# A fused attention and two-MLP kernel: the MLP part in a written order, one stream of weight steps, and shifted tile addresses

## The chip, the cores and the metric

One core of a Trainium2 chip runs the whole kernel in one launch. The metric is the device time of an execution in microseconds; the median of several executions is what counts. The profile shows one execution.

## The reference

```python
# attention: q, k, v are (2, 8, 768, 64); 4 sink columns, window 128
scores = q @ k^T / 8, kept where the column is a sink or 0 <= row - column < 128
a = softmax(scores);  x = a @ v, laid out as (1536, 512)
# first MLP: w_in (512, 2048), w_out (2048, 512)
h = x @ w_in;  g = h * sigmoid(1.702 * h);  x = g @ w_out
# second MLP: w_gate, w_val (512, 1536), w_out (1536, 512)
out = (sigmoid(x @ w_gate) * (x @ w_val)) @ w_out
```

The weights come as 64-bit floats in DRAM. The kernel reads them as pairs of 32-bit words.

## The kernel before, in words

**Three products for one.** Every MLP product is made in fp32r (a 32-bit type that TensorE takes in one pass) from a high and a low part: `mm3` (lines 147 to 151) issues hi by hi, hi by lo and lo by hi into one PSUM bank. A sum over the 512 contracted elements is 4 calls of `mm3`, 12 matmuls of 128 x 128 by 512 columns. This text calls such 12 matmuls a sum, and 4 sums (48 matmuls, one block by 512 tokens) a stage.

**Blocks.** The hidden width is walked in blocks of 512, the 1536 tokens in three blocks `tb` of 512. The first MLP has blocks i0, o0 to i3, o3 (`w_in`, `w_out`), the second g0, v0, p0 to g2, v2, p2 (`w_gate`, `w_val`, `w_out`): 17 blocks of four rows, 68 rows. A stage of an i-block is called h, of an o-block y, of a p-block o. In h, y, g and v stages the weights are the stationary operand; in o stages they are the moving one and the activations are stationary.

**A row of weights** (`weight_steps`, lines 104 to 131): a DMA of 512 KB into `raw` (two buffers); ACT takes the absolute value with a scale and an accumulator (line 118); DVE shifts (121), merges the sign (123) and the low bits (125); ACT casts to the high part `wh` (128); POOL subtracts to get the low part `wl` (130). The load of row i+2 is issued behind line 125 of row i, which frees its buffer.

**Where the blocks lie.** `load_w` gives block number k (in the order i0, o0, i1, o1, ..., p2) a buffer of `wpool` on the left side of SBUF where k mod 5 is 0 or 1, of `wpool2` on the right side otherwise. In the program as built, `wpool` begins at a multiple of 128 bytes of a partition. The right side is filled downwards: pool `acc` (29,344 bytes) begins at byte 200,000, which is 64 past a multiple of 128, and so do `tmp` below it and all tiles of `wpool2`. The blocks that lie in `wpool2` are i1, o1, i2, o3, g0, v0, v1, p1 and g2.

**Activations.** Behind an h sum ACT takes the sigmoid, DVE multiplies (line 461), ACT casts to `gh` (451), DVE subtracts to `gl` (453). A y stage uses them as the moving operand; DVE adds the sum into `yacc` (487). Behind a g and a v sum come a sigmoid (662), a multiplication (663) and the same split.

**The order.** The attention part runs under a manual schedule: strings `ORDER0` (units 0 to 9) and `ORDER` (from unit 10) say in which order the parts of a unit are issued, with a lag in units behind each letter. T transposes q and k, t copies the result to `kq`, S are scores, m the masked maximum, x the exponential, n the normalisation, P transposes probabilities and p copies them, K, k do so for the sinks, V multiplies with v, h and l split the result into `xh`, `xl`, H is a piece of the first h product, G a step of its activation, Y a sum of y, W a part of the weight steps, D a few dummy matmuls. T, P and K share a PSUM pool of two buffers (`ps_t`). A string `TAIL` orders the transition. From there the MLP part is left to the framework's scheduler, which orders the instructions of each engine by its own estimate.

**Stages.** `h_stage` makes its first sum, then calls `after`, which runs the y stage of the token block before, and goes on with its other three sums. `gv_stage` does the same with the o stage behind its first g and v sums.

Of the kernel before, what the change touches and what calls it, by code (L numbers as in the profile page):

```python
# [27 lines left out]
TAIL = "G4 H4 Y1 H4 G4 Y1 H4 G4 Y1 H4 G4 Y1 W3 G3 W3 Y1 G3 W3 Y1 G4 W4 Y1 G4 W4 G4 W4 G4"  # L28
I_FULL = 10
LOADS = (2, 3)  # L30
W_SEQ = [0, 0, 1, 3, 3, 3, 3, 3, 3, 3, 1]
# [22 lines left out]
def fast_path(ctx, tc, ident, nwv, any_, q, k, v, n_sink, window, w_in, w_out, w_gate, w_val, w_out2, out):  # L54
# [39 lines left out]
    def weight_block(src, nm, pool):  # L94

        wh = pool.tile([P, 4, 512], F32R, tag="wh", name=f"wh_{nm}")
        wl = pool.tile([P, 4, 512], F32R, tag="wl", name=f"wl_{nm}")

        def load(i):
            raw = stg.tile([P, 512, 2], I32, tag="raw", bufs=2, name=f"raw_{nm}_{i}")  # L100
            nc.sync.dma_start(raw, src[:, i, :].bitcast(I32).rearrange("p (f t) -> p f t", t=2))
            return raw, wh[:, i, :], wl[:, i, :], f"{nm}_{i}"

        return (wh, wl), [lambda i=i: load(i) for i in range(4)]

    def weight_steps(loads):


        raws = [load() for load in loads[:2]]
        yield  # L110
        for i in range(len(loads)):
            raw, h, l, nm = raws[i]
            lo, hi = raw[:, :, 0], raw[:, :, 1]
            w = stg.tile([P, 512], I32, tag="w", bufs=2, name=f"w_{nm}")
            wf = w.bitcast(F32)
            n = len(nbig)
            nbig.append(nm)
            nc.scalar.activation(wf, hi.bitcast(F32), AF.Abs, scale=2.0 ** -112,
                                 accum_out=big[:, n : n + 1])
            yield  # L120
            nc.vector.tensor_scalar(w, w, 3, None, ALU.logical_shift_left)
            yield
            nc.vector.scalar_tensor_tensor(w, hi, -0x80000000, w, ALU.bitwise_and, ALU.bitwise_or)
            yield
            nc.vector.scalar_tensor_tensor(w, lo, 29, w, ALU.logical_shift_right, ALU.bitwise_or)
            raws += [load() for load in loads[i + 2 : i + 3]]
            yield
            nc.scalar.copy(h, wf)  # L128
            yield
            nc.gpsimd.tensor_tensor(l, wf, f32(h), ALU.subtract)  # L130
            yield

    slots = [0]

    def load_w(src, nm):

        w = weight_block(src, nm, wpool if slots[0] % 5 < 2 else wpool2)
        slots[0] += 1
        return w
# [63 lines left out]
    wz = acc.tile([P, 512 + 16], mybir.dt.bfloat16, name="wz")  # L203
# [220 lines left out]
    def mlp_h():  # L424


        for g in range(len(blocks)):
            tb, off = divmod(g * QB, TB)
            ts_ = slice(off, off + QB)
            for f2 in range(GF // 2):  # L430
                pool, tag = h_banks[(g * GF // 2 + f2) % len(h_banks)]
                ps = pool.tile([P, 2, QB], F32, tag=tag, name=f"ha_{g}_{f2}")
                for i in range(2):
                    f = 2 * f2 + i
                    fs = slice(f * P, (f + 1) * P)
                    for kk in range(KD):
                        mm3(ps[:, i, :], wi[0][:, kk, fs], wi[1][:, kk, fs],
                            xh[tb][:, kk, ts_], xl[tb][:, kk, ts_], kk == 0, kk == KD - 1)
# [7 lines left out]
    def split(nm, src):  # L446
# [5 lines left out]
        yield  # L452
# [12 lines left out]
    def at_once(steps):  # L465
        while True:
            try:
                next(steps)
# [8 lines left out]
    def y_part(g, tb, wo, gs, d):  # L477
# [5 lines left out]
        ya = yacc[:, d, tb * TB : (tb + 1) * TB]  # L483
        if g == 0:
# [3 lines left out]


    first = [load_w(src, nm) for src, nm in ((in_block(w_in, 0), "i0"), (out_block(w_out, 0), "o0"))]  # L490
    wi = first[0][0]
    w_steps = weight_steps([load for _, loads in first for load in loads])
# [5 lines left out]
    W_ALL = 1 + 4 * 6  # L498
    w_done = [1]

    def w_some(n):
        piece(w_steps, n)
        w_done[0] += n
# [11 lines left out]

    parts = {"c": t_prev, "T": t_mm, "t": t_out, "S": s_mm, "m": s_max, "x": s_exp, "i": s_inv, "n": s_norm,
# [6 lines left out]
    piece(w_steps, 1)  # L523
# [3 lines left out]
    wo = first[1][0]  # L527

    def y0_steps():
        for tb in range(NTB):  # L530
            for d in range(KD):
                y_part(0, tb, wo, gs0[tb], d)
# [18 lines left out]
    with tc.manual_schedule(engines=engines):  # L551
        i = 0
        while nxt["l"] < len(units):
# [13 lines left out]
            for o in orders[which]:  # L567
                if o[0] == "H":

                    h_some(int(o[1:]), l_done // NPAIR if w_done[0] >= W_ALL else 0)  # L570
# [8 lines left out]
                elif o[0] == "W":  # L579
                    steps = W_SEQ[i] if i < len(W_SEQ) else 3  # L580
# [8 lines left out]
            if i == len(units):  # L589
                esq.close()  # L590
                g_pools.append(ctx.enter_context(tc.tile_pool(name="gpb", bufs=4)))
# [5 lines left out]
        piece(w_steps, 99)  # L597
# [5 lines left out]
        wpool2 = ctx.enter_context(tc.tile_pool(name="wpool2", bufs=3, side="right"))  # L603
        second = load_w(in_block(w_in, 1), "i1")
        w_steps = weight_steps(second[1])
        for o in TAIL.split():
            if o[0] == "H":
                h_some(int(o[1:]), len(blocks))
            elif o[0] == "W":
                piece(w_steps, int(o[1:]))  # L610
# [4 lines left out]
        for _ in h_steps:  # L615
            pass
        esg.close()
        for steps in (w_steps, silu0, y0):
            for _ in steps:
                pass  # L620
    ps_h = ctx.enter_context(tc.tile_pool(name="ps_h", bufs=4, space=PSUM))

    def load_w2(src, nm):
        w, loads = load_w(src, nm)
        for _ in weight_steps(loads):
            pass
        return w

    def h_stage(g, tb, wi, after):
        res = []  # L630
        for f in range(GF):
            ps = ps_h.tile([P, TB], F32, tag="h", name=f"h_{g}_{tb}_{f}")
            fs = slice(f * P, (f + 1) * P)
            for kk in range(KD):
                mm3(ps, wi[0][:, kk, fs], wi[1][:, kk, fs], xh[tb][:, kk, :], xl[tb][:, kk, :],
                    kk == 0, kk == KD - 1)
            res.append(at_once(silu_steps(g, tb, f, ps)))
            if f == 0:
                after()
        return res  # L640

    def y_stage(g, tb, wo, gs):
        for d in range(KD):
            y_part(g, tb, wo, gs, d)
            ya = yacc[:, d, tb * TB : (tb + 1) * TB]
            if g == NG1 - 1:
                nc.scalar.copy(xh[tb][:, d, :], ya)
                nc.vector.tensor_tensor(xl[tb][:, d, :], ya, f32(xh[tb][:, d, :]), ALU.subtract)

    def gv_stage(g, tb, wg, wv, after):  # L650
        res = []
        for f in range(GF):
            fs = slice(f * P, (f + 1) * P)
            pss = []
            for w, nm in ((wg, "g"), (wv, "v")):
                ps = ps_h.tile([P, TB], F32, tag="h", name=f"{nm}_{g}_{tb}_{f}")
                for kk in range(KD):
                    mm3(ps, w[0][:, kk, fs], w[1][:, kk, fs], xh[tb][:, kk, :], xl[tb][:, kk, :],
                        kk == 0, kk == KD - 1)
                pss.append(ps)  # L660
            sg = tmp.tile([P, TB], F32, tag="sg", name=f"sv_{g}_{tb}_{f}")
            nc.scalar.activation(sg, pss[0], AF.Sigmoid)  # L662
            nc.vector.tensor_tensor(sg, pss[1], sg, ALU.mult)  # L663
            res.append(at_once(split(f"v{g}_{tb}_{f}", sg)))
            if f == 0:
                after()
        return res

    oacc = acc.tile([P, NT // P, DM], F32, tag="yacc", name="oacc")

    def o_stage(g, tb, wo, gs):
        for j in range(TB // P):
            n = tb * (TB // P) + j
            ts_ = slice(j * P, (j + 1) * P)

            nd = 2 if g == NG2 - 1 and n == NT // P - 1 else 1
            for ds in (slice(i * DM // nd, (i + 1) * DM // nd) for i in range(nd)):
                ps = ps_y.tile([P, DM // nd], F32, tag="y", name=f"o2_{g}_{tb}_{j}_{ds.start}")
                for f in range(GF):
                    mm3(ps, gs[f][0][:, ts_], gs[f][1][:, ts_], wo[0][:, f, ds], wo[1][:, f, ds],  # L680
                        f == 0, f == GF - 1)
                oa = oacc[:, n, ds]
                if g == 0:
                    nc.scalar.copy(oa, ps)
                else:
                    nc.vector.tensor_tensor(oa, ps, oa, ALU.add)
                if g == NG2 - 1:
                    nc.sync.dma_start(out[n * P : (n + 1) * P, ds], oa)

    def check_inputs():  # L690

        fl = const.tile([P, 5], F32, name="fl")
        flag = const.tile([P, 1], F32, name="flag")
# [214 lines left out]
```

## Time and profile before

| what | value |
|---|---|
| median of 3 executions | 694.38 us (692.54 to 694.4) |
| profiled execution | 692.46 us |
| its span, first to last instruction | 690.7 us |
| PE busy in the span | 671.1 us (97%) |
| DVE, ACT, POOL busy | 395.3, 280.1, 154.1 us |
| DMA, mean rate | 71 GB/s |

PE is TensorE's matmul row. Matmuls are pipelined: one is shown as busy for about 0.39 us while the next starts 0.23 us behind it, so a busy PE says only that no gap opened. How fast it went is read from how many matmuls start in a stretch.

### The profile page before, as it was taken

The page shows a single profiled execution, that of the slowest core. Times are in us where ns is not written, and L with a number is a line of the kernel's source. Part 1 is how long each engine was busy: PE and PEld are TensorE (multiplying, and loading weights), DVE is VectorE, ACT ScalarE, POOL GpSimd, SP SyncE. Part 2 cuts the span into 40 slices and gives each one's busy share as a digit, 9 for nine tenths or more (in the row PEclk, how much of TensorE's full clock was granted, in tenths as well). Part 3 has the DMA queues.
Part 4 walks back from the last instruction along what each step waited for, and adds up shares of the span by engine and source line. Part 5 has one row for each costly group of instructions (what it writes and reads, how often), then busy time and mean ns, then how long its engine had stood idle before and what let it go on. Part 6 is the DMA issues. An engine that isn't in the chain of part 4 may idle for free.

```text
span 690.7 us, 9435 instructions
## 1 busy us (share of the span) xinstructions
PE 671.1 (97%) x3518; PEld 542.6 (79%) x3518; DVE 395.3 (57%) x792; ACT 280.1 (41%) x667; POOL 154.1 (22%) x235
## 2 busy tenths in 40 slices
PE   7899999999998999999999999999989999999996
PEld 3568888988886887888888888888868888888885
DVE  6987876567988889348856940206672325222222
ACT  4777766735535444234434532225441113111110
POOL 4656564103333331013102300003420002000000
PEclk9999999999999999999999999999999999999999
DMA  9855610013334434003300320002440000000101
GB/s 198 203 122 124 171 49 3 1 31 121 123 122 131 144 95 149 0 1 123 121 1 29 124 91 1 1 0 66 150 150 0 1 1 0 1 31 31 46 16 65
DMA packets 50150, 49.06 MB, mean 71 GB/s; under 512 B 39728, under 2 KB 39984, under 8 KB 50096
## 3 DMA queue, kind: packets, MB, share of 16 engines
q1 hardware_dynamic: 49264, 48.24, 24.3%
q8 instruction: 29, 0.48, 0.3%
q10 hardware_dynamic: 832, 0.13, 0.1%
q14 instruction: 25, 0.20, 0.1%
HBM read 45.22 MB, written 3.15 MB: 70 GB/s over the span
## 4 chain that ended last, share of the span: by engine, by line
PE 70%; DVE 15%; DMA 8%; ACT 4%; issue 2%; POOL 1%; SPq 0%; ACTq 0%; POOLq 0%; DVEq 0%
PE g L149 4%; PE o L149 4%; PE g L150 4%; PE o L151 4%; PE g L151 4%; PE o L150 4%; PE v L151 4%; PE v L150 4%; PE v L149 4%; PE o L408 4%; PE y L150 3%; PE y L151 3%; PE y L149 3%; PE s L314 3%; PE h L150 3%; PE h L151 3%
## 5 line engine op out<-in xcount | busy, mean ns | idle before, releaser
L663 DVE TENSOR_TENSOR sv<-v,sv 128x512 f32<-128x512 f32 x36 | 24.8, 689 | 114.4 <-PE v L151 114.3
L150 PE MATMUL y<-gl,wh_o 128*128 128x512 f32 x192 | 76.1, 397 | 1.3 <-DVE gl L453 1.3
L151 PE MATMUL y<-gh,wl_o 128*128 128x512 f32 x192 | 75.6, 395 | 0.0
L149 PE MATMUL y<-gh,wh_o 128*128 128x512 f32 x192 | 73.6, 398 | 1.7 <-ACT gh L451 1.7
L149 PE MATMUL o<-wh_p,gh_v 128*128 128x512 f32 (+1 forms) x148 | 57.0, 385 | 1.7 <-ACT gh_v L451 1.7
L662 ACT ACTIVATE sv<-g 128x512 f32<-128x512 f32 x36 | 21.5, 596 | 90.1 <-PE g L151 90.1
L150 PE MATMUL o<-wl_p,gh_v 128*128 128x512 f32 (+1 forms) x148 | 56.9, 384 | 0.0
L149 PE MATMUL g<-xh,wh_g 128*128 128x512 f32 x144 | 56.8, 394 | 0.0
L151 PE MATMUL v<-xh,wl_v 128*128 128x512 f32 x144 | 56.8, 394 | 0.0
L151 PE MATMUL o<-wh_p,gl_v 128*128 128x512 f32 (+1 forms) x148 | 56.7, 385 | 0.0
L150 PE MATMUL v<-xl,wh_v 128*128 128x512 f32 x144 | 56.7, 394 | 0.0
L151 PE MATMUL g<-xh,wl_g 128*128 128x512 f32 x144 | 56.7, 394 | 0.0
L150 PE MATMUL g<-xl,wh_g 128*128 128x512 f32 x144 | 56.7, 394 | 0.0
L149 PE MATMUL v<-xh,wh_v 128*128 128x512 f32 x144 | 56.7, 394 | 0.0
L151 PE MATMUL h<-xh,wl_i 128*128 128x512 f32 x144 | 56.7, 394 | 0.0
L150 PE MATMUL h<-xl,wh_i 128*128 128x512 f32 x144 | 56.7, 394 | 0.0
L149 PE MATMUL h<-xh,wh_i 128*128 128x512 f32 x144 | 56.7, 393 | 0.0
L451 ACT CAST gh_v<-sv 128x512 fp32r<-128x512 f32 x36 | 22.3, 620 | 79.0 <-DVE sv L663 78.8
L340 ACT ACTIVATE pr<-pr,nmax 128x272 f32<-128x272 f32 (+2 forms) x96 | 47.1, 494 | 15.1 <-DVE nmax L328 10.4
L355 POOL TENSOR_SCALAR pr<-pr,st 128x272 f32<-128x272 f32 (+2 forms) x96 | 44.5, 479 | 35.9 <-DVE st L346 19.8
L130 POOL TENSOR_TENSOR wl_p<-w_p,wh_p 128x512 fp32r<-128x512 f32 x12 | 16.4, 1372 | 153.9 <-ACT wh_p L128 153.9
L149 PEld LDWEIGHTS y<-gh,wh_o 128*128 128x128 f32 x192 | 36.5, 190 | 10.7 <-ACT gh L451 2.7
(138 smaller groups left out, 1465.8 us busy)
## 6 DMA issues: line engine op xcount, KB each, us to landing
raw_i<-in_moe_w_in_dram SPq DMA_DIRECT2D x16, 512.0 KB, 3.8
raw_o<-in_moe_w_out_dram SPq DMA_DIRECT2D x16, 512.0 KB, 3.3
raw_g<-in_moe_w_gate_dram SPq DMA_DIRECT2D x12, 512.0 KB, 3.4
raw_v<-in_moe_w_val_dram SPq DMA_DIRECT2D x12, 512.0 KB, 3.5
raw_p<-in_moe_w_out_dram SPq DMA_DIRECT2D x12, 512.0 KB, 3.2
v<-in_v_dram SPq DMA_DIRECT2D x12, 256.0 KB, 4.2
out_dram<-oacc SPq DMA_DIRECT2D x11, 256.0 KB, 2.0
k<-in_k_dram SPq DMA_DIRECT2D x10, 256.0 KB, 4.8
```

Of the source, the lines that this page charges most:

```text
L130: nc.gpsimd.tensor_tensor(l, wf, f32(h), ALU.subtract)
L149: nc.tensor.matmul(ps, ah, bh, start=first, stop=False)
L150: nc.tensor.matmul(ps, ah, bl, start=False, stop=False)
L151: nc.tensor.matmul(ps, al, bh, start=False, stop=last)
L314: nc.tensor.matmul(ss[j][:, :n], kq[p][hd, qsl], kq[p][hd, c0 : c0 + n], start=True, stop=True)
L340: nc.scalar.activation(pt, pt, AF.Exp, bias=nm[:, it : it + 1], scale=-1.0, accum_out=sts[u][:, 0, e, j : j + 1])
L355: nc.gpsimd.tensor_scalar(pt, pt, st[:, 1, e, j : j + 1], 1.0, ALU.mult, ALU.mult)
L408: nc.tensor.matmul(o[64 * j : 64 * j + 64, cs], vf(j), pf(j), start=i == 0, stop=i == len(steps) - 1)
L451: nc.scalar.copy(h, src)
L662: nc.scalar.activation(sg, pss[0], AF.Sigmoid)
L663: nc.vector.tensor_tensor(sg, pss[1], sg, ALU.mult)
```

## The change

- The MLP part is issued under the manual schedule too: `products_b` with `h_stage`, `y_stage`, `gv_stage`, `o_stage` is written out in the order in which the four engines get it.
- One generator, `weight_stream`, holds the steps of all 68 rows in order. `behind()` is called behind every sum (one call a sum) and advances it by 1, 1, 1, 2 groups in turn; a row has three groups. A block gets its buffer when block k-5 has been read, and the stream waits for that by yielding.
- From the tail on, the low part is subtracted on DVE (`SUB_B`), one row late.
- Behind an h sum the weight group stands between the cast to `gh` and the subtraction to `gl`. `h_stage` calls `after` behind its second sum.
- Blocks lie in five slots: two in `wpool`, one in the new `wpool3` (left side, opened when q and k are done), two in `wpool2`. i1 starts within the attention part.
- `wz` grows by 64 bytes, the tiles `st` from 64 to 128 bytes.
- `ORDER`, `ORDER0`, `TAIL`, `I_FULL` and `W_SEQ` change.

```diff
-ORDER = "W0 i-2 c-0 n-2 S0-1 S1-1 m0-1 m1-1 G2 x0-1 V-4 h-4 T-0 Y1 t-0 H1 l-4 P0-3 H1 W1 p0-3 P1-3 p1-3 H1 x1-1 K-3 k-3 W2 G2 H1"
-ORDER0 = "c-0 i-2 n-2 S0-1 S1-1 m0-1 m1-1 W0 x0-1 V-4 h-4 T-0 t-0 l-4 H1 P0-3 p0-3 W1 P1-3 p1-3 K-3 H1 H1 H1 x1-1 D4 k-3 W2"
-I_FULL = 10
+ORDER = "W0 S0-1 i-2 c-0 n-2 S1-1 m0-1 m1-1 G2 x0-1 V-4 h-4 T-0 Y1 t-0 P0-3 H1 H1 W1 p0-3 P1-3 l-4 p1-3 H1 x1-1 K-3 W2 k-3 G2 H1"
+ORDER0 = "c-0 i-2 n-2 D4 S0-1 S1-1 m0-1 m1-1 W0 x0-1 V-4 h-4 P0-3 T-0 t-0 l-4 H1 p0-3 W1 P1-3 p1-3 K-3 H1 H1 H1 x1-1 W2 k-3"
+TAIL = "G2 W1 G2 H8 G2 W1 G2 H4 W1 Y1 G2 W1 G2 H4 W1 Y1 G2 W1 G2 H4 W1 Y1 G2 W1 G2 H4 W1 Y1 G2 W1 G2 H4 W1 Y1 G3 W1 G1 Y1 G3 W1 G1 Y1 G3 W1 G1 Y1 G3 W1 G1"
+W_DRAIN = 4
+W_B = (1, 1, 1, 2)
+SUB_B = lambda nc: nc.vector
+I_FULL = 9
...
+    def weight_stream(blocks):
...
+        for n, (k, i) in enumerate(rows):
+            nm = blocks[k][0]
+            raw, w = raws.pop(n), ws[n]
+            lo, hi = raw[:, :, 0], raw[:, :, 1]
+            if n and late:
+                sub(n - 1)
+                yield n, False
             nc.vector.tensor_scalar(w, w, 3, None, ALU.logical_shift_left)
+            yield n, False
             nc.vector.scalar_tensor_tensor(w, hi, -0x80000000, w, ALU.bitwise_and, ALU.bitwise_or)
+            yield n, True
             nc.vector.scalar_tensor_tensor(w, lo, 29, w, ALU.logical_shift_right, ALU.bitwise_or)
+            load(n + 2)
+            yield n, True
+            if i == 0:
+                while k % 5 not in dict(w_pools) or (k >= 5 and blocks[k - 5][0] not in w_read):
+                    yield None
+                pool = dict(w_pools)[k % 5]
+                weights[nm] = [pool.tile([P, 4, 512], F32R, tag=t, name=f"{t}_{nm}") for t in ("wh", "wl")]
+            nc.scalar.copy(weights[nm][0][:, i, :], w.bitcast(F32))
+            late = sub_engine[0] is nc.vector
+            if not late:
+                yield n, False
+                sub(n)
+                yield n + 1, False
+            size(n + 1)
+            yield n + (not late), True
...
-    wz = acc.tile([P, 512 + 16], mybir.dt.bfloat16, name="wz")
+    wz = acc.tile([P, 512 + 48], mybir.dt.bfloat16, name="wz")
...
-            sts[u] = ap_.tile([P, 2, 2, 4], F32, tag="st", bufs=3, name=f"st_{nid(u)}")[:, :, :, :2]
+            sts[u] = ap_.tile([P, 2, 2, 8], F32, tag="st", bufs=3, name=f"st_{nid(u)}")[:, :, :, :2]
...
         nc.scalar.copy(h, src)
-        yield
+        yield "hi"
         nc.vector.tensor_tensor(l, src, f32(h), ALU.subtract)
...
+                if next(steps) == "hi":
+                    behind()
...
+        if 0 < g < NG1 - 1:
+            behind()
...
+    def behind():
+        w_group(W_B[sums[0] % len(W_B)])
+        sums[0] += 1
...
+            res.append(at_once(silu_steps(g, tb, f, ps)))
+            if f == (GF - 1 if (g, tb) == (1, 0) else 1):
+                after()
...
+                if nm == "g":
+                    nc.scalar.activation(sg, ps, AF.Sigmoid)
+                    behind()
+            nc.vector.tensor_tensor(sg, ps, sg, ALU.mult)
+            res.append(at_once(split(f"v{g}_{tb}_{f}", sg)))
+            if f == 0:
+                after()
...
-        wpool2 = ctx.enter_context(tc.tile_pool(name="wpool2", bufs=3, side="right"))
+        g_pools.append(ctx.enter_context(tc.tile_pool(name="gpb", bufs=4)))
+        wpool2 = ctx.enter_context(tc.tile_pool(name="wpool2", bufs=2, side="right"))
+        w_pools += [(3, wpool2), (4, wpool2)]
+        sub_engine[0] = SUB_B(nc)
...
+        products_b()
```

## Rows read from the trace of the kernel before

**Rows 1.** Page, part 1: busy time and instructions of each engine.

```profile
PE 671.1 (97%) x3518; PEld 542.6 (79%) x3518; DVE 395.3 (57%) x792; ACT 280.1 (41%) x667; POOL 154.1 (22%) x235
```

**Rows 2.** Windows, three stretches: busy (instructions) of PE, PEld, DVE, ACT, POOL; clock; DMA.

```profile
0.00:53.00 53.00, 44.56 (x353) 29.40 (x354) 41.37 (x163) 34.79 (x117) 30.26 (x77) 1.00 0.76 171
...
137.40:371.50 234.10, 231.12 (x1022) 188.29 (x1021) 172.34 (x252) 103.14 (x210) 50.95 (x36) 0.99 0.27 86
371.50:690.70 319.20, 311.00 (x1359) 252.93 (x1357) 121.63 (x178) 82.77 (x158) 32.27 (x24) 1.00 0.13 44
```

**Rows 3.** Windows of PE, undisturbed stages: y(o2), h(i3), h(i2), o(p0), o(p1).

```profile
286.25:297.15 10.90, 10.90 (x50) 1.00 0.00 0
319.10:329.98 10.88, 10.88 (x49) 1.00 0.43 143
252.08:263.28 11.20, 11.20 (x50) 1.00 0.44 115
410.70:421.60 10.90, 10.90 (x49) 1.00 0.01 2
545.80:556.80 11.00, 11.00 (x50) 1.00 0.00 0
```

**Rows 4.** The same view, stages with a wait: y(o1), y(o2), o(p1).

```profile
213.80:229.66 15.86, 13.39 (x50) 0.89 0.43 137
263.30:275.05 11.75, 11.24 (x50) 1.00 0.51 147
510.30:523.57 13.27, 11.54 (x49) 1.00 0.23 80
```

**Rows 5.** The same view, one sum of g1 between sums of v1.

```profile
493.70:496.45 2.75, 2.75 (x13) 1.00 0.42 167
```

**Rows 6.** Waits of PE: waiter, releaser, us in total, times, longest.

```profile
PE tp L370 <- DVE kq L301: 4.5, 8, 1.2
PE o L149 <- ACT gh_v L451: 1.7, 1, 1.7
```

**Rows 7.** Windows of PE: the stretch behind the wait at 214 us.

```profile
217.66:221.08 3.42, 3.42 (x8) 0.50 0.35 109
```

**Rows 8.** Timeline of ACT around 511 us.

```profile
511.07 0.66 ACT L118 ACTIVATE w_p<-raw_p 128x512 f32<-128x512 f32 x1 [2.65 <-DMA raw_p<-in_moe_w_out_dram]
...
513.64 0.62 ACT L451 CAST gh_v<-sv 128x512 fp32r<-128x512 f32 x1 [1.82 <-DVE sv L663]
```

**Rows 9.** Lines of DVE, 164 to 690 us: shapes, count, busy us, mean ns.

```profile
L125 DVE SCALAR_TENSOR_TENSOR w_g<-raw_g,w_g 128x512 int32<-128x512 int32 x12 | 11.6, 971 | 0.1
...
L123 DVE SCALAR_TENSOR_TENSOR w_p<-raw_p,w_p 128x512 int32<-128x512 int32 x12 | 8.2, 683 | 0.1
...
L121 DVE TENSOR_SCALAR w_i<-w_i 128x512 int32<-128x512 int32 x8 | 3.4, 424 | 3.7 <-ACT w_i L118 3.5
```

**Rows 10.** Timeline: a subtraction on POOL, and DVE's line 453 beside and behind it.

```profile
173.70 2.72 POOL L130 TENSOR_TENSOR wl_o<-w_o,wh_o 128x512 fp32r<-128x512 f32 x1 [3.99 <-ACT wh_o L128]
...
175.79 1.18 DVE L453 TENSOR_TENSOR gl<-sg,gh 128x512 fp32r<-128x512 f32 x1
...
179.62 0.68 DVE L453 TENSOR_TENSOR gl<-sg,gh 128x512 fp32r<-128x512 f32 x1
```

**Rows 11.** Timeline of PE: one attention unit.

```profile
42.90 0.44 PE L288 MATMUL tqk<-ident,k 128*128 128x128 f32 x2
...
43.40 0.60 PE L370 MATMUL tp<-ident,pr 128*128 128x128 f32 x4
44.41 0.66 PE L370 MATMUL tp<-ident,pr 128*128 128x128 f32 x4 [0.41 <-DVE kq L301]
...
45.01 0.60 PE L209 MATMUL wps<-wz 128*128 128x256 bf16 x4
```

**Rows 12.** Timeline of ACT, the same unit.

```profile
44.09 0.59 ACT L376 COPY pt<-tp 128x512 f32<-128x512 f32 x1 [0.70 <-PE tp L370]
```

**Rows 13.** Page, part 6: DMA issues, KB each, us to landing.

```profile
raw_g<-in_moe_w_gate_dram SPq DMA_DIRECT2D x12, 512.0 KB, 3.4
```

More of the change, by code (lines that the diff above doesn't have):

```diff
@@ L91, in fast_path @@
     nmax = const.tile([P, B * NQB * NPAIR, 4], F32, name="nmax")
[L94 to L104, printed above, removed]
@@ L106, in weight_steps @@
-    def weight_steps(loads):
-        raws = [load() for load in loads[:2]]
-        yield
-        for i in range(len(loads)):
-            raw, h, l, nm = raws[i]
-            lo, hi = raw[:, :, 0], raw[:, :, 1]
[L114 to L120, printed above, removed]
+    weights, w_pools, w_read = {}, [], set()
@@ new lines, in fast_path, with load, size, sub @@
+    sub_engine = [nc.gpsimd]
+    def weight_stream(blocks):
+        rows = [(k, i) for k in range(len(blocks)) for i in range(4)]
+        raws, ws = {}, {}
+        def load(n):
+            if n < len(rows):
+                k, i = rows[n]
+                nm, src = blocks[k]
+                raws[n] = stg.tile([P, 512, 2], I32, tag="raw", bufs=2, name=f"raw_{nm}_{i}")
+                nc.sync.dma_start(raws[n], src[:, i, :].bitcast(I32).rearrange("p (f t) -> p f t", t=2))
+        def size(n):
+            if n < len(rows):
+                k, i = rows[n]
+                ws[n] = stg.tile([P, 512], I32, tag="w", bufs=2, name=f"w_{blocks[k][0]}_{i}")
+                nc.scalar.activation(ws[n].bitcast(F32), raws[n][:, :, 1].bitcast(F32), AF.Abs,
+                                     scale=2.0 ** -112, accum_out=big[:, n : n + 1])
+        def sub(n):
+            k, i = rows[n]
+            h, l = (t[:, i, :] for t in weights[blocks[k][0]])
+            sub_engine[0].tensor_tensor(l, ws.pop(n).bitcast(F32), f32(h), ALU.subtract)
+        load(0)
+        load(1)
+        yield 0, True
+        size(0)
+        yield 0, True
+        for n, (k, i) in enumerate(rows):
+            nm = blocks[k][0]
+            raw, w = raws.pop(n), ws[n]
+            lo, hi = raw[:, :, 0], raw[:, :, 1]
+            if n and late:
+                sub(n - 1)
+                yield n, False
@@ L487, in y_part @@
             nc.vector.tensor_tensor(ya, ps, ya, ALU.add)
-    first = [load_w(src, nm) for src, nm in ((in_block(w_in, 0), "i0"), (out_block(w_out, 0), "o0"))]
-    wi = first[0][0]
-    w_steps = weight_steps([load for _, loads in first for load in loads])
+    w_blocks = []
+    for g in range(NG1):
+        w_blocks += [(f"i{g}", in_block(w_in, g)), (f"o{g}", out_block(w_out, g))]
+    for g in range(NG2):
+        w_blocks += [(f"g{g}", in_block(w_gate, g)), (f"v{g}", in_block(w_val, g)),
+                     (f"p{g}", out_block(w_out2, g))]
+    w_pools += [(0, wpool), (1, wpool)]
+    w_steps = weight_stream(w_blocks)
+    w_rows = [0]
     def piece(steps, n):
@@ L496, in piece, with w_step, w_group, w_need @@
             next(steps, None)
-    W_ALL = 1 + 4 * 6
-    w_done = [1]
-    def w_some(n):
-        piece(w_steps, n)
-        w_done[0] += n
+    def w_step():
+        state = next(w_steps, None)
+        if state is None:
+            return True
+        w_rows[0] = state[0]
+        return state[1]
+    def w_some(n):
+        for _ in range(n):
+            w_step()
+    def w_group(n):
+        for _ in range(n):
+            while not w_step():
+                pass
+    def w_need(nm):
+        k = [b for b, _ in w_blocks].index(nm)
+        while w_rows[0] < 4 * (k + 1):
+            state = next(w_steps)
+            assert state is not None, nm
+            w_rows[0] = state[0]
+            print("late", nm)
+        return weights[nm]
     h_banks = [(ps_m, "m")]
@@ new lines, in fast_path, with o_stage @@
+    oaccs = []
+    def o_stage(g, tb, gs):
+        if not oaccs:
+            oaccs.append(acc.tile([P, NT // P, DM], F32, tag="yacc", name="oacc"))
+        wo = w_need(f"p{g}")
+        for j in range(TB // P):
+            n = tb * (TB // P) + j
+            ts_ = slice(j * P, (j + 1) * P)
+            nd = 2 if g == NG2 - 1 and n == NT // P - 1 else 1
+            for ds in (slice(i * DM // nd, (i + 1) * DM // nd) for i in range(nd)):
+                ps = ps_y.tile([P, DM // nd], F32, tag="y", name=f"o2_{g}_{tb}_{j}_{ds.start}")
+                for f in range(GF):
+                    mm3(ps, gs[f][0][:, ts_], gs[f][1][:, ts_], wo[0][:, f, ds], wo[1][:, f, ds],
+                        f == 0, f == GF - 1)
+                behind()
+                oa = oaccs[0][:, n, ds]
+                if g == 0:
+                    nc.scalar.copy(oa, ps)
+                else:
+                    nc.vector.tensor_tensor(oa, ps, oa, ALU.add)
+                if g == NG2 - 1:
+                    nc.sync.dma_start(out[n * P : (n + 1) * P, ds], oa)
+        if tb == NTB - 1:
+            w_read.add(f"p{g}")
@@ new lines, in flag_out, with y0_rest, products_b, second @@
+    def flag_out():
+        tot = ps_y.tile([1, 1], F32, tag="y", name="tot")
+        nc.tensor.matmul(tot, flags[0], nc.const_aps.tensor(1.0, [P, 1], F32), start=True, stop=True)
+        nc.vector.tensor_copy(any_, tot)
+    def y0_rest():
+        for steps in (silu0, y0):
+            for _ in steps:
+                pass
+        w_read.add("o0")
+    def products_b():
+        todo = [(y0_rest,)]
+        def second():
+            while todo:
+                f, *a = todo.pop(0)
+                f(*a)
+        for g in range(1, NG1):
+            for tb in range(NTB):
+                gs = h_stage(g, tb, second)
+                todo.append((y_stage, g, tb, gs))
+            w_read.add(f"i{g}")
+        for g in range(NG2):
+            for tb in range(NTB):
+                gs = gv_stage(g, tb, second)
+                todo.append((o_stage, g, tb, gs))
+                if g == NG2 - 1 and tb == 0:
+                    check_inputs()
+                if g == NG2 - 1 and tb == 1:
+                    flag_out()
+            w_read.update((f"g{g}", f"v{g}"))
+        second()
@@ L614, in fast_path @@
                 y_some(int(o[1:]))
-        for _ in h_steps:
-            pass
+        h_some(GF * KD * len(blocks) - h_done[0], len(blocks))
+        w_read.add("i0")
         esg.close()
[L618 to L688, printed above, removed]
```

127 lines of the change are left out of this document (64 added, 63 removed).

## The prediction

> **What bounds the kernel now.** The page's first part comes first: PE is busy for 97% of the span, the other engines for at most 57% [rows 1]. That number alone does not tell whether PE has anything to give, since each matmul is shown as busy while the next one runs. The windows by stage do. Up to 53 us PE is busy for 44.56 us of 53; from 137 us on it is busy nearly throughout [rows 2], so there the question is how fast one matmul follows another. In windows laid on whole stages, 48 matmuls and one or two at the edges, three stages take 10.88 to 10.90 us, one takes 11.20 and one 11.00 [rows 3]. That is 226.9 ns a matmul against 233.3 and 229.2, at a full clock, with no wait in them. What tells them apart is the buffer: o2, i3 and p0 lie in `wpool`, i2 and p1 in `wpool2`. The DMA share is no reason, since the fast h(i3) has 0.43 and the slow h(i2) 0.44.
>
> Then the waits. PE's list is short [rows 6], but three stages are longer than their kind: 15.86, 11.75 and 13.27 us [rows 4]. [...] Where such a wait comes from is seen on ACT: line 118 starts at 511.07 behind a wait of 2.65 us for a DMA, and the cast on which PE's o stage waits follows at 513.64 [rows 8]. ACT takes its instructions in order, so a weight step put ahead of its data holds up the activations behind it.
>
> So there are two things to win in the MLP part: the spacing of matmuls whose operand lies 64 bytes off, and a handful of waits. The attention part has the waits of P's transposes, 4.5 us in 8 [rows 6].
>
> **The change part by part. Addresses.** `acc` grows by 64 bytes and is filled downwards from the same end, so it begins at 199,936 = 1562 x 128, and `tmp` and `wpool2` below it move to multiples of 128 too. Three tiles `st` of 128 bytes in place of 64 take 192 bytes more, so the pools below `st` move by 256 and keep their offsets. `wpool3` and the second activation pool stand on the left, where all sizes are multiples of 128. Stationary blocks that lay 64 off: i1, o1, i2, o3, g0, v0, v1, g2, eight blocks of three stages: 24 x (11.20 - 10.90) = 7.2 us [rows 3]. The moving block p1: 3 x (11.00 - 10.90) = 0.3 us. The aligned blocks g1 and v2 alternate with an unaligned one sum by sum, and such a sum takes 2.75 us [rows 5] against 10.90 / 4 = 2.72: 24 sums x 0.03 = 0.7 us. Together **8.2 us**; bounds 0 (if the offset is not the cause, below) and 8.7 (24 stages against 10.88). In the attention part `pt` and `psk`, the moving operands of V's 384 matmuls, move from 64 to 0: at p1's price, 0.10 us in 48, that is 2.1 ns each or 0.8 us; the first 53 us are not bound by PE alone, so I take **0.4** (bounds 0 and 0.8).
>
> [...]
>
> **The waits in the MLP part.** What they cost: 15.86 - 11.20 = 4.7, 11.75 - 10.90 = 0.85, 13.27 - 11.00 = 2.3, together **7.8 us** [rows 3, 4]. Does the new order remove them? The load of row n+2 is issued in the second group of row n and its data are wanted in the third group of row n+1, four groups later. A sum advances one or two groups, so at least three sums, 3 x 2.72 = 8.2 us, lie between, and the DMA lands in 3.4 [rows 13]. The wait for DMA on ACT goes. The y stage now starts behind two sums of the next h, not one: its first sum wants the last activation in its last quarter, 2 x 2.72 + 2.0 = 7.5 us behind the sum that makes it (before: 4.8). The chain is a sigmoid (as long as the cast), a product (0.68), a cast (0.62 [rows 8]), a weight group or two on DVE (1.8 to 2.5) and the subtraction (0.68): 4.4 to 5.1 us. It fits. I take all 7.8 (bounds 3 and 7.8).
>
> **The low parts on DVE.** Eleven of 68 subtractions are still on POOL in the attention part, 57 go to DVE, at the 0.68 us of a like instruction [rows 9, 10]: 39 us of DVE time. From 137 to 371 us DVE is busy for 172.3 of 234.1 us [rows 2]; POOL's 36 instructions there become 36 x 0.68 = 24.5 more, 197 in 234, or 84%. Behind that it is 121.6 + 24 x 0.68 = 138 in 319, or 43%. Some is given back: beside a subtraction on POOL line 453 takes 1.18 us, behind it 0.68 [rows 10], and line 125 has a mean of 971 ns for one block where line 123 has 683 for another [rows 9]. The densest stretch is the last block of the first MLP, where every sum brings DVE two instructions of 0.68 us (product and subtraction behind h, addition and `xl` behind y), 1.36, and 1.25 weight groups, that is 1.25 / 3 of a row's 0.68 + 0.42 + 0.68 + 0.68 = 2.46 us, 1.0: 2.4 in the 2.72 that PE takes. It is hidden, at **nothing**. If that cover were gone, every 0.1 us over 2.72 would cost 2.4 us in the 24 sums of that block. [...]
>
> **The attention part.** P's first transposes now precede T, so P's second set waits for ACT's copy of the first and no longer for DVE's copy of T. In the unit shown V ends at 42.90 and P takes 0.60 us; ACT would start 0.09 behind it, as it does now (44.00 to 44.09), take 0.59, and the second set start near 44.22, not 44.41 [rows 11, 12]. That is 0.19 a unit, 1.5 in eight. In units where ACT is still at its exponentials the copy comes later, so I take half, 0.7. `I_FULL` of 9 drops one set of dummy matmuls, 0.5 to 0.6 us on PE [rows 11]: 0.5. Together **1.2 us** (bounds: 5.0 with all 4.5 us of waits gone, and a loss of 1.5 if each of eight units loses the 0.19). The weight steps of i1 move into the attention part, behind POOL and DVE work that has room from 53 us on, where PE has no idle time to lose; the two loads that come earlier pass no other transfer on SP that is wanted then.
>
> **New waits.** Twelve blocks wait for a buffer in the stream, and a block takes 9.6 calls (four rows of 2.4). The tightest, p1, gets its buffer at the start of g1's first token block and is used 14 calls later. In the last third of `TAIL` a sum of 2.72 us brings DVE four steps of an activation (1.36), a group (0.82) and a copy (0.68), 2.86, for four sums. I add **0.5 us** (bounds 0 and 5: two waits like that at 512 us).
>
> **Sum.** 692.46 - 8.2 - 0.4 - 7.8 - 1.2 + 0.5 = 675.4 us against the profiled execution. That one and one of the three timed (692.54) lie together, the other two 1.9 us higher, and the median is one of those; I put the median at **676.0**.
>
> **Rivals.** *Waits in other places* (0.16). A fixed order cannot step around a late operand: a weight group on ACT whose DVE step is late holds the sigmoid behind it. For it: two such holds are seen now [rows 4, 8]. Against it: 8.2 us of lead against 3.4. Two or three of them at 2.3 us and one with a clock drop at 4.7 give 5 to 8 us back: 681 to 684.
>
> *The offset is not the cause* (0.06), but that `wpool2` stands on the right side. All stationary blocks on that side are 64 off, so the rows can't exclude it. For the offset speaks that the moving block p1 costs a third as much. Then i1, o3 and v1, which leave that side, gain 9 x 0.3 = 2.7 us at most, and the rest of the 8.2 stays: 681 to 684.
>
> *Slower* (0.03): ACT stands in line 118 for every row's DMA. Point: a row is four groups ahead; if a load took over 8.2 us plus the 2.4 us of slack in the activations' chain, each of 57 rows would pass its wait on to PE. From 17 / 57 = 0.3 us a row the whole gain is gone; at 0.5 it is 676 + 28 = 704. Now loads land in 3.4 us [rows 13].
>
> *More* (0.05): the waits of the attention part go entirely: 676 - 3.8 = 672 and lower.
>
> **How the numbers follow.** The forecast, 672 to 680, has 0.70. The range reaches from 671.5 (attention's bound) to 682 (some waits back); it leaves out the lower end of "more", the upper part of the first rival, the second and the slower one. A difference of 0.3%, 2.1 us, is what a measurement of this kernel can tell. All cases but the slower one are faster by more than that: 0.95, with 0.02 for the same and 0.03 for slower.
>
> **What would show it.** Right: all h, y, g, v and o stages of the changed kernel take 10.9 us; no wait of PE over 1 us behind 140 us; clock 1.00 throughout; POOL idle in the MLP part with DVE's means back at 0.68. Wrong: stages of 11.2 us for blocks in `wpool2`; ACT waiting for `raw` DMAs while PE waits for `gh`; DVE without idle time between 330 and 370 us; P's waits as long as before.

## The result, and the profile after

The changed kernel takes **676.38 us** (median of 4 executions, 676.25 to 676.88), the kernel before 693.46 on the same chip (4 executions, 691.55 to 694.4): a ratio of 0.976, 95% interval 0.9741 to 0.9778. The forecast was 676.0. Faster, by 17.1 us.

The profiled execution took 676.37 us and its span is 674.2. The page's first part, busy time and instructions of each engine, answers to [rows 1]; below it is the head of the chain that ended last:

```profile
PE 658.9 (98%) x3514; PEld 541.3 (80%) x3514; DVE 398.4 (59%) x849; ACT 277.6 (41%) x667; POOL 76.0 (11%) x178
...
PE 93%; DMA 2%; ACT 2%; DVE 1%; SPq 0%; issue 0%; ACTq 0%; DVEq 0%
```

PE's share hardly moved, as a busy PE says little; in the chain PE has 93% where it had 70% before. Two stretches (busy time and instructions of PE, PEld, DVE, ACT, POOL; clock; DMA share; GB/s), to be read against [rows 2]; they are the first MLP with the transition, and the rest:

```profile
137.40:362.04 224.64, 224.64 (x1020) 187.11 (x1019) 162.19 (x267) 95.88 (x194) 0.00 (x0) 1.00 0.24 75
362.04:674.20 312.16, 305.40 (x1359) 252.76 (x1357) 130.06 (x216) 84.67 (x164) 0.00 (x0) 1.00 0.16 50
```

The clock is 1.00 in both, POOL does nothing, and PE has no gap in the first stretch. Then the windows on whole stages (PE's columns, clock, DMA), here y(o1) of the second token block, the one that took 15.86 us before, h(i2), o(p0) and o(p1):

```profile
215.15:226.03 10.88, 10.88 (x49) 1.00 0.30 98
269.56:280.44 10.88, 10.88 (x49) 1.00 0.28 90
400.12:411.00 10.88, 10.88 (x49) 1.00 0.47 146
498.04:508.92 10.88, 10.88 (x49) 1.00 0.39 125
```

y(o1) was 15.86 and o(p1) 13.27 [rows 4], h(i2) 11.20 [rows 3]. Nearly every stage of the MLP part behind the transition now takes 10.88 us, 226.7 ns a matmul. What the traces show of fp32r's one pass is its pace: in the kernel before, an fp32r matmul of 128x256 at 53.52 us is followed by the next in 0.11 us, and the bf16 dummies of 128x256 at 45.01 are 0.11 us apart too. PE's list of waits (waiter, releaser, us in total, times, longest) answers to [rows 6]:

```profile
PE tp L394 <- ACT pt L400: 2.5, 5, 1.0
PE tp L394 <- DVE kq L325: 2.0, 3, 1.1
PE wps L233 <- DVE wz L228: 1.2, 1, 1.2
PE tqk L312 <- DMA q<-in_q_dram: 1.2, 2, 1.0
PE s L338 <- DVE kq L325: 1.0, 2, 0.7
...
PE ts L408 <- POOL sk L383: 0.2, 1, 0.2
...
PE o L432 <- DVE xl L446: 0.2, 1, 0.2
```

No y or o stage of the MLP part is in it (the `o` of L432 is V's). P's transposes, which waited 4.5 us in 8 for `kq`, still wait 4.5 us in 8, now for two releasers.

**Where the 16.1 us between the profiled executions lie.** The distances from the start of each h, y, g, v and o matmul of the MLP part, the first h product left out (2315 in each trace), to the next start on PE sum to 539.2 us before and 522.7 after: **16.5 us**, of which about 7.8 are the three stages with a wait, each over its own kind [rows 3, 4], and the other 8.7 the spacing. The last V of the attention part starts at 132.80 before and 132.53 after: 0.3 us for that part. Against that, 0.7 us more lie behind the last matmul and outside the span (6.76 + 2.17 us where it was 6.46 + 1.76).

### The profile page after: what moved, and what is told of

It reads as the page before. It is cut to its first block, busy times and chain, and to the rows that moved or that the text cites. A ratio compares the mean times of both kernels' runs of the same rounds, so it can differ in the third digit from the quotient of the medians.

```text
span 674.2 us, 9404 instructions
## 1 busy us (share of the span) xinstructions
PE 658.9 (98%) x3514; PEld 541.3 (80%) x3514; DVE 398.4 (59%) x849; ACT 277.6 (41%) x667; POOL 76.0 (11%) x178
## 4 chain that ended last, share of the span: by engine, by line
PE 93%; DMA 2%; ACT 2%; DVE 1%; SPq 0%; issue 0%; ACTq 0%; DVEq 0%
PE y L174 6%; PE y L173 6%; PE y L175 6%; PE g L173 5%; PE o L173 5%; PE o L175 5%; PE h L174 5%; PE v L173 5%; PE g L175 5%; PE h L173 5%; PE o L174 5%; PE v L175 5%; PE g L174 5%; PE v L174 5%; PE h L175 5%; PE o L432 4%
## 5 line engine op out<-in xcount | busy, mean ns | idle before, releaser
L175 PE MATMUL o<-wh_p,gl_v 128*128 128x512 f32 (+1 forms) x148 | 56.8, 383 | 0.0
L173 PE MATMUL o<-wh_p,gh_v 128*128 128x512 f32 (+1 forms) x148 | 56.8, 383 | 0.0
L476 ACT CAST gh<-sg 128x512 fp32r<-128x512 f32 x48 | 29.8, 622 | 49.6 <-DVE sg L486 49.6
L486 DVE TENSOR_TENSOR sg<-h,sg 128x512 f32<-128x512 f32 x36 | 24.8, 688 | 32.1 <-ACT sg L484 32.1
```

Of the source, the lines that this page charges most:

```text
L173: nc.tensor.matmul(ps, ah, bh, start=first, stop=False)
L175: nc.tensor.matmul(ps, al, bh, start=False, stop=last)
L476: nc.scalar.copy(h, src)
L486: nc.vector.tensor_tensor(sg, ps, sg, ALU.mult)
```

## The experiments

Each is one edit, of the kernel before (the first) or of the changed one. "The kernel before" stands for its median in the same batch: 693.62 us for the first four, 693.55 for the next four, 692.54 for the three after that, 694.63 for the last. The changed kernel was run in two batches, with medians of 676.38 and 677.24 (experiment 11); a median less than 1 us from these is not told apart from it.

**1. The addresses alone** (in the kernel before).

```diff
-wz = acc.tile([P, 512 + 16], ...)        -"st": [P, 2, 2, 4]
+wz = acc.tile([P, 512 + 48], ...)        +"st": [P, 2, 2, 8]
```

> The kernel before with the two widened tiles alone (wz by 64 bytes, st to 128 bytes), its order untouched: wpool2 begins at a multiple of 128. Theory (the offset of the operand sets the spacing): the 27 stages of the nine wpool2 blocks fall from 11.20 or 11.00 us to 10.9, and the kernel gains 8.2 to 8.7 us, some 685 us; the three waits stay. Rival (the right side of SBUF is the cause): the stages stay at 11.20 us and the time at that of the kernel before.

689.19 us (687.81 to 689.74), ratio 0.9936 [0.9913, 0.9959]: 4.4 us, half of what was expected. Windows of PE, first h(i2) and o(p1) without a wait, then y(o1) with its wait, the stretch with a low clock in it, y(o2), and the other o(p1):

```profile
251.81:262.69 10.88, 10.88 (x49) 1.00 0.37 108
541.99:552.87 10.88, 10.88 (x49) 1.00 0.00 0
...
212.97:230.05 17.08, 14.39 (x49) 0.80 0.42 132
216.00:222.80 6.80, 5.84 (x14) 0.50 0.30 93
262.69:274.99 12.30, 11.76 (x50) 1.00 0.50 143
506.19:520.23 14.04, 11.41 (x49) 1.00 0.24 77
```

The spacing is what was expected: blocks that still lie in `wpool2`, on the right side, run at 10.88. The offset is the cause and the side is not. But the three stages are now 6.2, 1.4 and 3.2 us over 10.88, 10.8 in all; before, they were 7.8 over their own kinds. In o(p1) the wait itself grew: PE idles for 14.04 - 11.41 = 2.6 us, before for 1.7 [rows 4]. In y(o1) PE idles hardly longer (2.7 us, before 2.5), and what grew is the stretch at a clock of 0.50, 6.8 us where it was 3.42 [rows 7]. That a PE which gets there sooner waits longer for operands made at the old pace fits o(p1); for the others it is not shown. The MLP part as a whole is 5.8 us shorter (its distances sum to 533.4 us, not 539.2), the profiled execution 4.7; the rest, about 1 us, is lost outside it.

**2 and 3. The order with operands at 64 or at 96 bytes past a multiple of 128** (in the changed kernel).

```diff
 order_only                                 offset_96
-wz = acc.tile([P, 512 + 48], ...)         -wz = acc.tile([P, 512 + 48], ...)
+wz = acc.tile([P, 512 + 16], ...)         +wz = acc.tile([P, 512 + 64], ...)
-"st": [P, 2, 2, 8]
+"st": [P, 2, 2, 4]
```

> The changed kernel with wz and st as before, so that wpool2 lies 64 bytes off again; order, stream and low parts as changed. Now i2, o1, g0, v0, p1 and g2 lie there. Theory: five stationary blocks at 15 x 0.32 us, p1 at 3 x 0.12, the sums of v2 between those of g2 at 12 x 0.03: 4.8 + 0.4 + 0.4 = 5.5 us more than the changed kernel, about 682 us, with no wait of PE in the MLP part. Rival (side of SBUF): 676 us, as the changed kernel.

682.12 us (681.77 to 683.03), ratio 0.983 [0.9807, 0.9853], 5.7 us over the changed kernel. Windows of PE on y(o1), h(i2) and o(p1):

```profile
194.59:205.78 11.19, 11.19 (x49) 1.00 0.27 93
272.26:283.46 11.20, 11.20 (x49) 1.00 0.25 87
503.31:514.31 11.00, 11.00 (x49) 1.00 0.38 126
```

The order alone takes every wait out of the MLP part. It also leaves fewer blocks in `wpool2`, so the offset costs it less than it cost the kernel before.

> The changed kernel with wz another 32 bytes wider: acc, and with it all right-hand pools, at 96 past a multiple of 128 in place of 0. Theory (any offset from 128 costs the same): stages of the wpool2 blocks at 11.20 us, some 682 us, as with 64. Rival (lines of 64 bytes, so that 96 is worse than 64): stages over 11.3 us and 684 us or more. Second rival (side): 676 us.

681.93 us (2 executions, 681.47 and 682.4), ratio 0.9829 [0.9799, 0.9859]. The same view, y(o1) and o(p1):

```profile
193.52:204.71 11.19, 11.19 (x49) 1.00 0.28 94
501.99:513.19 11.20, 11.20 (x49) 1.00 0.40 125
```

Weights as stationary operand cost the same at 96 as at 64, 6.5 ns a matmul over 226.7; as the moving one they cost 6.7 ns at 96 and 2.5 at 64. Of the offsets tried only the multiple of 128 is free. In all runs the other operand of these matmuls lies at a multiple of 128, so whether the offset itself counts or the difference between the two operands is not shown.

**4. The low parts back on POOL.**

```diff
-SUB_B = lambda nc: nc.vector
+SUB_B = lambda nc: nc.gpsimd
```

with the stream's last subtraction left out in this case, since on POOL no row is one late.

> The changed kernel with the low parts of the weights subtracted on POOL throughout, each in its own row, as in the kernel before. Theory (the order and the lead of the loads removed the waits, DVE has room either way): no wait over 0.5 us in the MLP part, time within 1 us of the changed kernel, though DVE's instructions beside POOL's stretch to some 1 us. Rival (POOL's hold on DVE made the waits): the PE waits for gh or gl come back, 2 to 8 us more.

675.89 us (675.87 to 676.32), ratio 0.9742 [0.972, 0.9764]: not told apart from the changed kernel, and no wait in the MLP part. What POOL does to DVE is seen in the lines of DVE from 137.4 to 362 us (shapes, count, busy us, mean ns, idle before). With POOL:

```profile
L487 DVE TENSOR_TENSOR sg<-yacc,sg 128x512 f32<-128x512 f32 x8 | 6.5, 812 | 0.8 <-ACT sg L485 0.6
...
L141 DVE TENSOR_SCALAR w_o<-w_o 128x512 int32<-128x512 int32 x12 | 6.1, 512 | 0.7 <-ACT w_o L119 0.7
L141 DVE TENSOR_SCALAR w_i<-w_i 128x512 int32<-128x512 int32 x8 | 5.5, 691 | 3.8 <-ACT w_i L119 3.8
```

In the changed kernel:

```profile
L486 DVE TENSOR_TENSOR sg<-yacc,sg 128x512 f32<-128x512 f32 x8 | 5.5, 686 | 0.8 <-ACT sg L484 0.8
...
L141 DVE TENSOR_SCALAR w_o<-w_o 128x512 int32<-128x512 int32 x12 | 5.1, 421 | 0.0
L141 DVE TENSOR_SCALAR w_i<-w_i 128x512 int32<-128x512 int32 x8 | 3.4, 424 | 0.0
```

Line 141, the shift, goes from 421 to 512 and from 424 to 691 ns (for `w_g` from 423 to 824), and eight products of the transition (`sg<-yacc,sg`) from 686 to 812; lines 143 and 145 keep their 692 and 684 ns. In the written order one DVE step of a row pays for POOL; before, the pairs fell as the scheduler placed them, and lines 123 and 125 paid too (up to 953 ns for `w_o`, and 971 for `w_g` [rows 9]). In the changed kernel it is not on PE's path.

**5. The y stage behind one sum of the next h, not two.**

```diff
-            if f == (GF - 1 if (g, tb) == (1, 0) else 1):
+            if f == (GF - 1 if (g, tb) == (1, 0) else 0):
```

> The changed kernel with h_stage calling the y stage behind its first sum, as before, in place of the second. Theory (the slack of the activations' chain matters): the last activation is wanted 4.8 us behind its sum, its chain takes 4.4 to 5.1 us, so y stages of the first MLP show waits of 0.1 to 0.6 us each for gl or gh, 1 to 4 us in all: 677 to 680 us. Rival (the lead of the loads and the pacing alone removed the waits): no such wait, 676 us.

677.1 us (677.0 to 678.12), ratio 0.9762 [0.974, 0.9784]. Two y stages have a wait (windows of PE):

```profile
233.96:245.30 11.34, 11.22 (x50) 1.00 0.31 92
299.72:311.02 11.30, 11.18 (x50) 1.00 0.33 93
```

They are 0.46 and 0.42 us over their kind, 0.9 in all, for `gl`: in the first, DVE starts its subtraction at 235.77 and the matmul that takes it starts at 236.51. The second sum is worth about that, just under the 1 to 4 us expected.

**6. Three weight groups behind every sum**, a row each, until the buffers are full.

```diff
-W_B = (1, 1, 1, 2)
+W_B = (3, 3, 3, 3)
```

> The changed kernel with a whole row of weights behind every sum (three groups in place of 1, 1, 1, 2), so that rows come in bursts wherever a buffer is free and the load has about 3.6 us of lead where the DMA needs 3.4. Theory (pace and lead removed the waits): DVE gets 1.36 + 2.46 = 3.8 us of work a sum of 2.72 in a burst and ACT waits for DMA again; PE waits for gh or gl come back, 5 to 20 us: 681 to 696. Rival (it is the fixed order as such): no waits, 676 us.

701.13 us (700.28 to 704.41), ratio 1.012 [1.0087, 1.0153]: slower than the kernel before, with the same instructions in another rhythm, and beyond the 681 to 696 that were expected. Windows of PE on y(o1), o(p1) and a stretch of low clock in it:

```profile
215.00:233.54 18.54, 13.60 (x49) 0.82 0.28 91
512.13:532.45 20.32, 14.66 (x49) 0.75 0.23 78
516.80:527.00 10.20, 7.01 (x16) 0.50 0.31 104
```

What is ahead of the activations is seen in DVE's timeline of that o(p1) (start, duration, instruction):

```profile
513.66 0.69 DVE L125 TENSOR_TENSOR wl_v<-w_v,wh_v 128x512 fp32r<-128x512 f32 x1
514.32 0.43 DVE L141 TENSOR_SCALAR w_v<-w_v 128x512 int32<-128x512 int32 x1
514.78 0.69 DVE L143 SCALAR_TENSOR_TENSOR w_v<-raw_v,w_v 128x512 int32<-128x512 int32 x1
515.51 0.69 DVE L145 SCALAR_TENSOR_TENSOR w_v<-raw_v,w_v 128x512 int32<-128x512 int32 x1
516.12 0.68 DVE L617 TENSOR_TENSOR sv<-v,sv 128x512 f32<-128x512 f32 x1
```

and in ACT's:

```profile
516.83 0.62 ACT L476 CAST gh_v<-sv 128x512 fp32r<-128x512 f32 x1 [2.54 <-DVE sv L617]
```

The picture is that of [rows 8], a cast of `gh_v` that starts late, but no load is behind it: ACT's waits for a weight DMA behind 140 us come to 0.3 us, where the expectation had them back. Four weight steps stand on DVE ahead of the product `sv`; ACT's cast waits for it, PE for the cast (3.2 us the longest), and then the clock falls to 0.50. The pace makes the waits, with no load late.

**7. The start's dummy matmuls behind T, not ahead of the scores.**

```diff
-ORDER0 = "c-0 i-2 n-2 D4 S0-1 ... P0-3 T-0 t-0 ..."
+ORDER0 = "c-0 i-2 n-2 S0-1 ... P0-3 T-0 D4 t-0 ..."
```

> The changed kernel with the four dummy matmuls of units 0 to 8 between T and the second set of P's transposes, where PE waits for ACT's copy, in place of ahead of S. Theory (in those units PE sets the pace, and its wait of 0.2 to 1 us at P can cover the 0.5 us of dummies): 1 to 3 us less, 673.5 to 675.5. Rival (ACT and DVE set the pace there): no change, 676 us.

676.3 us (675.7 to 676.94), ratio 0.9743 [0.9722, 0.9764]: no difference. From 25 to 55 us PE is busy for 28.04 us where the changed kernel shows 27.01, and unit 11's first scores start at 54.96 against 54.84. The dummies behind T cost nothing, so PE's gaps there are room.

**8. The attention part's old order**, all four strings of before: `ORDER`, `ORDER0`, `I_FULL = 10` and the `W_SEQ` that ends `3, 3, 3, 1`.

> The changed kernel with ORDER, ORDER0, I_FULL and W_SEQ of before. Theory (the traces show the new order one unit's worth of 1.05 us ahead at the last unit's S): 0.5 to 1.2 us more, 677 to 677.6. Rival (what it wins up to unit 23 is lost in the drain whatever the order): no change within 0.3 us.

678.48 us (678.25 to 678.7), ratio 0.9777 [0.9756, 0.9797]: 2.1 us over the changed kernel, more than the 0.5 to 1.2 expected. 1.3 of them are there when unit 23's first scores start (118.07 against 116.77); in the drain behind it, up to the last V, it takes 16.40 us against 15.76. Part of the 1.3 is the clock at the start: from 8 to 11 us it is 0.52 here and 0.50 in experiment 1, which has the old order too, and 1.00 in the changed kernel. Windows of PE in that stretch, experiment 1:

```profile
8.00:11.00 3.00, 3.00 (x15) 0.50 1.29 230
```

The profiled execution of before had 1.00 there, with the old order, so this is not the order's in every execution.

**9. No weight steps in the drain.**

```diff
-W_DRAIN = 4
+W_DRAIN = 0
```

> The changed kernel with W_DRAIN of 0: no weight step in the four units of the drain (116 to 133 us); what it would do there follows in the tail and behind the sums. Theory (i1's weight steps on DVE and POOL hold up V and the sink transpose of the last units, which cost 0.8 us between the last S and the last V): that stretch falls back from 15.76 to about 15.0 us, 0.5 to 0.8 us less, some 675.7 us. Rival (the order of P, T and l does it): no change there, 676.4 us or, where o1 then comes late, 1 to 2 us more.

677.41 us (677.07 to 679.55), ratio 0.9795 [0.9768, 0.9822]. Unit 23's scores and the last sinks of V in PE's timeline of the changed kernel:

```profile
116.77 1.19 PE L338 MATMUL s<-kq 64*128 64x272 f32 x8
...
132.16 0.63 PE L432 MATMUL o<-psk,vsk 128*64 128x128 f32 x8
```

and of this one:

```profile
116.81 1.19 PE L338 MATMUL s<-kq 64*128 64x272 f32 x8
...
131.20 0.63 PE L432 MATMUL o<-psk,vsk 128*64 128x128 f32 x8
```

15.39 us against 14.39: the steps of i1 cost the drain 1.0 us. But the rows left out then come late in the MLP part. Its y(o1) (window of PE) is

```profile
192.44:204.57 12.13, 11.45 (x49) 1.00 0.30 90
```

1.25 us over its kind, with a wait for `wh_o` of 0.61 us at 195.25. Gain and loss cancel.

**10. No dummy matmuls** (`D4` struck from `ORDER0`).

> The changed kernel without the four dummy matmuls a unit in units 0 to 8 (those at the start stay). Theory (ACT and DVE set the pace there, as the dummies behind T cost nothing): no change within 0.5 us. Rival (PE sets the pace): 9 x 0.5 us, up to 3 us less. Second rival (the clock falls without them): granted clock of 0.5 somewhere ahead of 53 us and 1 us or more on top.

677.86 us (677.24 to 678.63), ratio 0.9788 [0.9766, 0.981], 0.6 over the changed kernel in the same batch (experiment 11). Eight score matmuls in the start take 1.65 us (PE's timeline),

```profile
15.46 1.65 PE L338 MATMUL s<-kq 64*128 64x128 f32 x8 [0.78 <-DVE kq L325]
```

where the changed kernel takes 0.93:

```profile
13.40 0.93 PE L338 MATMUL s<-kq 64*128 64x128 f32 x8 [0.66 <-DVE kq L325]
```

Unit 3's scores start at 19.59, not 17.12. The matmuls take 1.8 times as long. Two transposes of k ahead of them (13.57) take 0.69 us, as they do in experiment 1 at 9.52, where the clock reads 0.50; in the changed kernel (11.64) they take 0.44. But the clock row reads 1.00 here, so that it was the clock is likely and not shown. From unit 3 to unit 11 it takes 37.2 us, no longer than the others.

**11. The changed kernel once more**, unedited, for what two traces of one program differ by.

> The changed kernel once more, on the same chip as the two runs beside it: 676.4 us, within 0.5. Any difference to the first profile within the attention part tells how far such differences between the experiments can be read.

677.24 us (676.15 to 679.77), ratio 0.9789 [0.9757, 0.9821]. Unit 11's scores start at 55.60, not 54.84: 0.76 us of difference within the first 55 us, so a smaller one there can't be read from one trace.

**12. Dummies only in the first three units, and half the weight steps in the drain.**

```diff
-W_DRAIN = 4
+W_DRAIN = 2
...
-                    warm(int(o[1:]), 256)
+                    if i < 3:
+                        warm(int(o[1:]), 256)
```

> The changed kernel with the dummy matmuls in units 0 to 2 alone and W_DRAIN of 2. Theory: from S of unit 3 to S of unit 11 about 37.2 us, as without dummies, in place of 37.7 to 38.7; S of unit 3 by 17.2 us, since the early dummies stay; the drain between 14.75 and 15.75 us; and no wait in the MLP part, since o1 has eight steps more than with none in the drain: 0.5 to 1.5 us less than the changed kernel, some 675.5 us. Rival (the loads of the first 50 us set the pace whatever PE does): within 0.5 us of the changed kernel.

677.63 us (5 executions, 675.02 to 677.85), ratio 0.9755 [0.9736, 0.9773]. Its profiled execution is the shortest of all, with the last matmul's end at 666.28 (the changed kernel: 667.44), but three of five executions lie at 677.6 to 677.9. It can't be told apart from the changed kernel. The drain takes 15.21 us, as expected; from unit 3 to unit 11 it takes 38.0, not the 37.2 expected.

## Why the prediction was right, and where it was not

**Addresses: 8.2 predicted, 8.7 measured.** Experiment 1 has the blocks still on the right side and at 10.88, which settles the rival on the side. In experiments 1 to 3 a stage takes 10.88 us with its block at a multiple of 128, 11.19 to 11.20 with a stationary block at 64 or 96.

**`pt` and `psk`: 0.4 predicted, 0 measured.** From unit 11's first scores to unit 23's, where half of V's matmuls lie, it takes 61.93 us before, 61.92 with the addresses alone and 61.93 in the changed kernel. The price of p1, an fp32r stage with PE bound, did not carry over to V's fp32 matmuls.

**Waits in the MLP part: 7.8 predicted, all gone, no new one.** The rivals that put waits elsewhere did not come. That a weight step ahead of its data holds up the activations is seen in the trace of before. The g sum whose activation is the late `gh_v` of [rows 8] ends at 502.16; its sigmoid starts on ACT at 507.83, behind the two weight casts and two steps of line 118 (one idle for 1.22 us until its DMA) and the cast of the activation before (idle for 1.24). The wait of 2.65 us for a DMA came to the cast by way of DVE: the product `sv` had both operands at 508.41 and started at 512.93, behind a shift that waited 1.47 us for line 118. Of the two reasons given, the runs bear out the second. The first was the lead of a load over its use. ACT's wait for weight DMAs behind 140 us did go, from 38.1 us in all to none, but experiment 6 brings PE's waits back, and larger, with next to no wait for a load. The second was that the activations' chain, with a weight group or two in it, fits into the time that it has; with a whole row in it (experiment 6) it does not. No run shortens the lead and keeps the pace, so how much of the 7.8 us was the lead's stays open. By medians, the addresses alone win 4.4 us and the order alone 11.5, together 15.9 against the 17.1 for both. In the MLP part the two add up: 5.8 and 10.8 us (the distances sum to 533.4 and 528.5) against 16.5.

**Low parts on DVE: nothing predicted, nothing measured** (experiment 4). DVE's load was overestimated: 84% and 43% worked out, 162.19 / 224.64 = 72% and 130.06 / 312.16 = 42% measured. The means are back at 0.68 to 0.69 us, and the estimate had only added instructions and taken none of the stretch away. It had also left i1's steps in the first stretch, ahead of which most of them now lie: DVE has 267 instructions there, 15 more than before [rows 2] and not 36.

**The attention order: 1.2 predicted, 0.3 measured** between the two profiles, which is less than two traces of the changed kernel differ by (experiment 11). This is the term that was mis-sized, and its mechanism was not borne out: P's waits come to 4.5 us as before, one of the prediction's own signs of being wrong, the copy of P taking the place of the copy of T as releaser in five of eight. That the new strings win something all the same is seen in experiment 8, where the old ones cost the changed kernel 2.1 us. Up to unit 11's scores the changed kernel is 1.05 us ahead of before; ten profiles with the new `ORDER0` or near it lie at 54.3 to 56.0 (the middle at 54.9), the one without dummies at 56.8, three with the old at 55.9 to 56.2, so about 1 us is likely won in the start. That the dummies ahead of the scores do it by the clock fits two of the three old profiles, with 0.50 and 0.52 from 8 to 11 us where all others show 1.00, but it is not shown: before's own profile, the third, had 1.00. From unit 11 to 23 nothing is won in any run.

The drain, from unit 23's scores to the last V, gave back 0.78 us (14.98 to 15.76). The prediction let i1's weight steps move there at no cost, behind POOL and DVE work with room. Experiment 9 shows that they cost 1.0 in the new order. Where, is seen in the timelines of DVE and POOL of the changed kernel there:

```profile
122.36 0.43 DVE L141 TENSOR_SCALAR w_i<-w_i 128x512 int32<-128x512 int32 x1 [0.49 <-ACT w_i L119]
122.83 0.69 DVE L143 SCALAR_TENSOR_TENSOR w_i<-raw_i,w_i 128x512 int32<-128x512 int32 x1
123.44 0.16 DVE L369 TENSOR_SCALAR st<-st 128x4 f32<-128x4 f32 x1
...
124.01 0.96 POOL L379 TENSOR_SCALAR pr<-pr,st 128x272 f32<-128x272 f32 x2 [2.84 <-DVE st L370]
```

and of experiment 9:

```profile
121.84 0.16 DVE L369 TENSOR_SCALAR st<-st 128x4 f32<-128x4 f32 x1
...
122.41 0.96 POOL L379 TENSOR_SCALAR pr<-pr,st 128x272 f32<-128x272 f32 x2 [2.69 <-DVE st L370]
```

Two weight steps, with a wait for ACT's step ahead of them, stand on DVE before the unit's `st`, so `st` and the normalisation on POOL that waits for it come 1.6 us later, and PE's list gets its small waits for `sk` and `xl`. DVE and POOL had room there on average; what counted was the place of the steps in the order.

**Sum.** 675.4 was worked out for the profiled execution, 676.37 measured. The difference of some 1.0 us is +0.4 (`pt`, `psk`), +0.9 (attention), +0.7 (behind the last matmul and outside the span), -0.5 (addresses), -0.5 (the new waits that did not come): the total was met in part because small errors cancel.

## What to carry to other kernels

Place the operands of long fp32r matmul streams at multiples of 128 bytes of a partition (64 and 96 past one cost 2.5 to 6.7 ns a matmul over 226.7 here), and check it on the built addresses by the time of undisturbed stages. Where background work stands in the same written order of an engine as a critical chain, its pace decides: a little behind every sum cost nothing, a whole row behind every sum cost 25 us (701.13 against 676.38). With the addresses alone the three slow stages got slower (10.8 us over their kind, not 7.8), so look at what a removed limit does to the waits behind it before judging it by the time.

## What the hardware showed that was not expected

- The price of an offset depends on the operand's role: 64 and 96 bytes cost a stationary block the same 6.5 ns a matmul of 512 columns, while a moving block pays 2.5 ns at 64 and 6.7 ns at 96.
- V's fp32 matmuls showed no such price at 64 bytes (61.93 us for twelve units in both).
- A wait on PE can cost more than itself: in experiment 6 the o(p1) stage is 9.4 us over its kind, of which 5.7 us are gaps (20.32 - 14.66), and 10.2 us of it run at a clock of 0.50.
